# Logits of the dilated local attention by block-diagonal matmuls on TensorE in place of a key gather on GpSimd

## The chip, the cores and the metric

The kernel runs on one core of a Trainium2 chip. The metric is the device time of one execution in microseconds (us), the median of several runs. PE is TensorE (PEld its weight loads), DVE is VectorE, ACT is ScalarE, POOL is GpSimd and SP is the engine whose queue issues most DMAs. The profile is of one execution; the median comes from other executions.

## The reference

Two attention blocks over the same input of 2048 tokens and 512 columns, with 32 heads of 16, are mixed by a gate for each token. A is full attention. B looks at 8 keys a query: the query's own position and every second one before it.

```python
x = A_x
g = _sigmoid((x * gate_w).sum(-1, keepdims=True))
a = _A_ref(x, A_wqkv, A_wo)          # softmax(q k^T / 4) v, 32 heads, then @ wo
b = _B_ref(x, B_wqkv, B_wo)
return g * a + (1 - g) * b

# in _B_ref
W, dil = 8, 2
idx = pos[:, None] - off[None, :]    # off = arange(W) * dil
mask = idx >= 0
kg = k[:, :, idx_c, :].reshape(B, H, S, W, Dh)
vg = v[:, :, idx_c, :].reshape(B, H, S, W, Dh)
logits = jnp.einsum("bhsd,bhswd->bhsw", q, kg) * scale
logits = jnp.where(mask[None, None, :, :], logits, -1e9)
attn = _softmax(logits, axis=-1)
o = jnp.einsum("bhsw,bhswd->bhsd", attn, vg)
```

## The kernel before

**Attention A** fills most of the time. Its work is cut into 32 periods: 4 chunks of 512 queries (`QW`) by 8 groups of 4 heads. A period has 64 units, each one key tile of 128 by one head by 512 queries. Most units go in sets of 3 and 2 in turn: score matmuls into one of two PSUM rings (`qk`), one exponential on ACT over the set (`ex`, `pT<-ring`), then the product with the values on PE (`pv_run`). There are 1709 such units; "unit" below means one of them. Another 339 units have their exponentials on DVE (`d_set`): `p1` makes a 16-bit number from the PSUM score, and two adds over three units at once, `raise1` (1536 columns) and `raise2` (3072 columns), shift it in SBUF between four products. Their buffers are `pd_a` and, later, `wall`. PE also makes A's keys, queries and values from `xT`, and runs matmuls on a zero tile (`z`) where the order would leave it with little to do.

**Attention B** goes in 16 tiles of 128 tokens (`b_tile`, line 881). PE projects keys, values and queries of a tile (12 matmuls of 512 columns); DVE evicts keys and values into `kvs`, which SP writes to `kv_scr` in DRAM, and the queries, scaled, into `qb`. SP then loads, for each query in its partition, 4 of its 8 keys at a time (`ksh`), twice, and likewise the values (`vsh`). POOL makes the logits: 8 multiplications of 512 columns (`logits_mul`), three rounds of halving sums (`logits_add`) and a last sum (`logits_out`) for each pair of keys. The softmax follows: maximum on DVE (`sm_pre`), subtraction on POOL (`sm_sub`), exponential on ACT (`sm_exp`), sum and reciprocal on DVE (`sm_post`), the factor 1 - g and the product on POOL (`sm_gate`, `sm_mul`). POOL multiplies by the values (`av_mul`, 8 a tile), accumulating DMAs and POOL add the parts (`av_sum`, `av_last`), PE transposes the result (`fin`), and DVE writes it to `obt` (`oe`). For each chunk PE then multiplies `obt` and A's result by the two output matrices (`ab_part`), DVE evicts and SP writes the output.

**The order** of each engine is fixed when the program is built. `op` records every operation with an engine, an assumed length, a due time, what it depends on (`deps`), what it must follow (`after`), and the buffers it takes (`alloc`) and uses (`use`); `list_schedule` plays them through and writes out one order for each engine, which the engine then keeps. `CFG` gives B's due times: `b_start` and `b_space` place the tiles. So a wait of one instruction holds back all that stands behind it on its engine. Small PSUM results share three banks (`misc`). Every POOL, DVE, ACT and SP instruction is recorded by one helper, so the profile gives them all line 364, and most of PE's line 373; groups are told apart by the names of their tiles.

Of the kernel before, what the change touches and what calls it, by code (L numbers as in the profile page):

```python
# [21 lines left out]
    b_start=36.0,  # L22
    b_space=(43.0,) * 4 + (45.0,) * 4 + (47.0,) * 8,
# [17 lines left out]
NGA = 3  # L41
# [56 lines left out]
NPR = 3  # L98
# [21 lines left out]
FIN, QB, KB, WO = 52.0, 0.0, 0.0, 26.0  # L120
# [181 lines left out]
def kernel(  # L302
# [103 lines left out]
    for t in range(NT):  # L406
        BT.append(BT[-1] + cfg["b_space"][t])
    UNIT = 0.465
# [62 lines left out]
    kv_scr = tc.dram_tile([16 + S, 2 * D], BF16, name="kv_scr")  # L471
# [26 lines left out]
    omg = const.tile([128, NT], FP32, name="omg")  # L498
    e1, d1 = av[:, 1, 0:NT], av[:, 1, NT:2 * NT]
# [31 lines left out]
    def init_pool3():  # L531
        zst["z"] = work.tile([128, 2 * D], BF16, name="kvs", tag="kvs", bufs=2)
        G.memset(zst["z"][0:16, :], 0.0)
# [11 lines left out]
    def load_x(sc):  # L545
        def s():
            xl = work.tile([128, W // 2, D], BF16, name="xld", tag="gat", bufs=NGA) if sc < NGA else stage
# [25 lines left out]
    xtok = [tok("gat", NGA) if sc < NGA else tok("dt", NDT) for sc in range(NC)]  # L573
# [8 lines left out]
    o_bw = op("sp", 1.0, load_bw, -8.3, lat=19.0)  # L582
    o_zr = op("sp", 0.6, load_zero, -8.2, deps=[o_wz], use=[zt], lat=19.0)
# [287 lines left out]
    o_g = op("dve", 0.8, zgate, GT + 6, deps=[a])  # L871
    a = op("pe", 1.2, zrows, GT + 8, full=1, deps=[o_g, o_init_p], alloc=[tzr])
# [6 lines left out]
    HB = D  # L879

    def b_tile(t):
        st = {}
        tb = BT[t]
        cb, tl = t // TPC, t % TPC
        rel = max(24.0, tb - 70.0)

        def proj(key, off, c0):
            def s():
                if c0 == 0:
                    st[key] = misc_ps([128, D])  # L890
                    if key == "pk":
                        st["kvs"] = work.tile([128, 2 * D], BF16, name="kvs", tag="kvs", bufs=2)
                    if key == "pq":
                        st["qb"] = work.tile([128, D], BF16, name="qb", tag="qb", bufs=2)
                for c in range(c0, c0 + 2):
                    mm_ct(st[key], xT[:, c, t * 128:(t + 1) * 128], bw[:, c, off * D:(off + 1) * D], c == 0, c == DC - 1)
            return s
        tkv = tok("kvs", 2)

        def ke():  # L900
            V.tensor_copy(out=st["kvs"][:, 0:D], in_=st["pk"][:])

        def ve():
            V.tensor_copy(out=st["kvs"][:, D:2 * D], in_=st["pv"][:])

        def kvd():
            SP.dma_start(out=kv_scr[16 + t * 128:16 + (t + 1) * 128, :], in_=st["kvs"][:])
        tk = tok("misc", 2)
        a = op("pe", WAVE(2), proj("pk", 1, 0), tb - 34 - KB, full=2, deps=[o_bw] + o_xt[cb], alloc=[tk, tkv], rel=rel)
        a = op("pe", WAVE(2), proj("pk", 1, 2), tb - 33.5 - KB, full=2, deps=[a], use=[tk])  # L910
        ka = op("dve", 0.61, ke, tb - 33 - KB, deps=[a], use=[tk, tkv])
        tk = tok("misc", 2)
        a = op("pe", WAVE(2), proj("pv", 2, 0), tb - 32 - KB, full=2, deps=[o_bw] + o_xt[cb], alloc=[tk], rel=rel, after=[a])
        a = op("pe", WAVE(2), proj("pv", 2, 2), tb - 31.5 - KB, full=2, deps=[a], use=[tk])
        va = op("dve", 0.61, ve, tb - 31 - KB, deps=[a, ka], use=[tk, tkv])
        o_kvd.append(op("sp", 0.6, kvd, tb - 30 - KB, deps=[va], use=[tkv], lat=3.0))

        tqb = tok("qb", 2)

        def qe():  # L920
            V.tensor_scalar(out=st["qb"][:], in0=st["pq"][:], scalar1=float(DH) ** -0.5, scalar2=None, op0=ALU.mult)
        tk = tok("misc", 2)
        a = op("pe", WAVE(2), proj("pq", 0, 0), tb - 24 - QB, full=2, deps=[o_bw] + o_xt[cb], alloc=[tk, tqb], rel=rel)
        a = op("pe", WAVE(2), proj("pq", 0, 2), tb - 23.5 - QB, full=2, deps=[a], use=[tk])
        qa = op("dve", 0.61, qe, tb - 23 - QB, deps=[a], use=[tk, tqb])

        def load(key, off, hf):
            def s():
                r0 = 16 + t * 128 - DIL * hf * WH
                base = kv_scr[r0:r0 + 128, off * D:(off + 1) * D]  # L930
                st[key, hf] = work.tile([128, WH, D], BF16, name=key, tag="gat", bufs=NGA)
                SP.dma_start(out=st[key, hf][:], in_=_ap(base, [[2 * D, 128], [-DIL * 2 * D, WH], [1, D]]))
            return s
        tks, tvs = [tok("gat", NGA), tok("gat", NGA)], [tok("gat", NGA), tok("gat", NGA)]
        tlg, tbb = tok("lg", 2), tok("obb", 1)
        kvd_ = o_kvd[max(0, t - 1):t + 1] + [o_zr]
        lk = [op("sp", 0.7, load("ksh", 0, hf), tb + KL[hf], deps=kvd_, alloc=[tks[hf]], lat=7.0) for hf in range(2)]
        lv = [op("sp", 0.7, load("vsh", 1, hf), tb + (18, 30)[hf], deps=kvd_, alloc=[tvs[hf]], lat=7.0) for hf in range(2)]

        def logits_mul(hf, wp, w_, c0):  # L940
            def s():
                if hf == 0 and wp == 0 and w_ == 0 and c0 == 0:
                    st["lg"] = work.tile([128, H, W], FP32, name="lg", tag="lg", bufs=2)
                if w_ == 0 and c0 == 0:
                    st["prod", hf, wp] = work.tile([128, WP, D], FP32, name="prod", tag="prod", bufs=NPR)
                G.tensor_tensor(out=st["prod", hf, wp][:, w_, c0:c0 + HB], in0=st["ksh", hf][:, wp + w_, c0:c0 + HB],
                                in1=st["qb"][:, c0:c0 + HB], op=ALU.mult)
            return s, "bb", HB

        def logits_add(hf, wp, n, w0, ws):  # L950
            def s():
                pv_ = st["prod", hf, wp][:].rearrange("p w (h d) -> p w h d", d=DH)
                G.tensor_tensor(out=pv_[:, w0:w0 + ws, :, 0:n], in0=pv_[:, w0:w0 + ws, :, 0:n],
                                in1=pv_[:, w0:w0 + ws, :, n:2 * n], op=ALU.add)
            return s, "ff", ws * H * n

        def logits_out(hf, wp):
            def s():
                lg = st["lg"]
                pv_ = st["prod", hf, wp][:].rearrange("p w (h d) -> p w h d", d=DH)  # L960
                w0 = hf * WH + wp
                G.tensor_tensor(out=lg[:, :, w0:w0 + WP].rearrange("p h w -> p w h"),
                                in0=pv_[:, :, :, 0], in1=pv_[:, :, :, 1], op=ALU.add)
# [87 lines left out]
        def chain_ops(seq, dls, alloc, toks):  # L1051

            made, tps, a, seen = {}, {}, None, set()
            for n_, (g_, k_, (f, kind, n), src, deps) in enumerate(seq):
                new = g_ not in tps
                if new:
                    tps[g_] = tok("prod", NPR)
# [432 lines left out]
```

## Time and profile before

| what | value |
|---|---|
| median of 3 runs | 842.53 us (841.78 to 843.44) |
| the profiled execution's own time | 844.3 us |
| its span, first to last instruction | 842.5 us |
| mean granted TensorE clock | 0.985 |
| first exponential of A begins | 19.54 us |
| ACT, exponentials of A (684) | 782.0 us |
| DVE / POOL busy | 668.4 / 669.4 us |
| PE matmuls on the zero tile | 403 |
| DMA queue of SP: packets, MB | 52,752, 54.05 |

The span lies within the profiled execution's time. Busy times of PE come from matmuls that overlap, so they are not added up as shares. An instruction's idle time stands with the group that waited, and behind the arrow stands what ended the wait. Since all engines keep a written order, an idle time shows where the order and the real lengths part.

### The profile page before, as it was taken

To read this page: it belongs to the slowest core of one execution; us is meant where nothing else is said; L and a number is where in the kernel's file an instruction comes from. 1 tells how busy PE (TensorE), PEld (TensorE's weight loads), DVE (VectorE), ACT (ScalarE), POOL (GpSimd) and SP (SyncE) were. 2 spreads that over 40 slices of the span, in tenths; PEclk is the share of its full clock that TensorE was granted. 3 is DMA by queue.
4 is the path that set the end of the run, shared out by engine and by line. 5 is a ranking of instruction groups with operands and counts; after the bars stand their busy time and mean duration, and the time that the engine had idled before them with its cause. 6 is when DMAs were issued, how large, how long until landed. Compare 5 with 4: busy or idle time off the path is not lost.

```text
span 842.5 us, 17539 instructions
## 1 busy us (share of the span) xinstructions
PE 763.5 (91%) x6947; PEld 243.6 (29%) x7000; DVE 668.4 (79%) x967; ACT 789.7 (94%) x706; POOL 669.4 (79%) x710
## 2 busy tenths in 40 slices
PE   8999899998989888998899998989989999999996
PEld 4333333233222222222222222222222222223322
DVE  5556987868775788999988689988788889887775
ACT  3999989997999899999999999999989999999995
POOL 3197979998799885799979998988898996999400
PEclk9999999998999899999999999999999999999998
DMA  7402171534361705236042625342342516120000
GB/s 252 139 29 86 36 179 58 132 103 87 98 153 55 171 2 101 88 113 162 27 120 69 167 60 139 86 125 67 91 86 88 138 38 166 48 76 2 1 2 25
DMA packets 58882, 77.18 MB, mean 92 GB/s; under 512 B 3744, under 2 KB 50848, under 8 KB 58800
## 3 DMA queue, kind: packets, MB, share of 16 engines
q1 hardware_dynamic: 52752, 54.05, 20.6%
q0 software_dynamic: 6048, 22.02, 14.1%
q8 instruction: 54, 0.88, 0.5%
q14 instruction: 28, 0.23, 0.1%
HBM read 43.78 MB, written 10.26 MB: 64 GB/s over the span
## 4 chain that ended last, share of the span: by engine, by line
ACT 38%; PE 29%; issue 17%; DVE 14%; DMA 1%; ACTq 0%; SPq 0%; DVEq 0%
ACT pT L364 37%; PE misc_ps L373 20%; PE ring L373 8%; DVE pd_a L364 6%; DVE wall L364 6%; DMA xld<-in_A_x_dram 1%; DVE qa L364 1%; DVE kvs L364 0%; PE pxt L621 0%; DVE kt_all L364 0%; DVE vd_all L364 0%; DVE qs L364 0%; DVE vp_all L364 0%; ACT lg L364 0%; DVE qb L364 0%
## 5 line engine op out<-in xcount | busy, mean ns | idle before, releaser
L364 ACT ACTIVATE pT<-ring 128x1536 bf16<-128x1536 f32 (+1 forms) x684 | 782.0, 1289 | 35.2 <-PE ring L373 28.2
L373 PE MATMUL ring<-qt,kt_all 32*128 32x512 bf16 x1709 | 273.2, 385 | 39.2 <-ACT pT L364 32.5
L373 PE MATMUL misc_ps<-pT,vp_all 128*17 128x512 bf16 (+1 forms) x1709 | 217.2, 387 | 0.4
L364 POOL TENSOR_TENSOR prod<-ksh,qb 128x512 f32<-128x512 bf16 x128 | 170.9, 1364 | 41.4 <-DMA ksh<-kv_scr 34.0
L364 POOL TENSOR_TENSOR prod<-prod 128x512 f32<-128x512 f32 (+2 forms) x192 | 187.6, 977 | 3.2
L373 PEld LDWEIGHTS <-kt_all 32*128 32x128 bf16 x2048 | 85.7, 91 | 299.1 <-issue 290.6
L364 DVE TENSOR_SCALAR pd_a<-pd_a 128x1536 uint16<-128x1536 uint16 (+1 forms) x130 | 153.4, 1180 | 15.3 <-PE misc_ps L373 14.2
L364 DVE TENSOR_SCALAR pd_a<-misc_ps 128x512 uint16<-128x512 f32 x195 | 130.6, 680 | 39.7 <-PE misc_ps L373 36.8
L373 PE MATMUL misc_ps<-z 128*32 128x512 bf16 x403 | 133.4, 393 | 1.9 <-DVE z L364 1.6
L364 DVE TENSOR_SCALAR wall<-wall 128x1536 uint16<-128x1536 uint16 x96 | 121.5, 1271 | 16.8 <-PE misc_ps L373 16.2
L373 PE MATMUL misc_ps<-qt,kt_all 32*128 32x512 bf16 x339 | 124.9, 384 | 7.6 <-DVE pd_a L364 4.4
L364 DVE TENSOR_SCALAR wall<-misc_ps 128x512 uint16<-128x512 f32 x144 | 95.4, 682 | 17.4 <-PE misc_ps L373 13.5
L373 PEld LDWEIGHTS <-vp_all 128*17 128x17 bf16 (+1 forms) x2048 | 57.8, 88 | 85.9 <-issue 70.0
L364 POOL TENSOR_TENSOR prod<-vsh,lg 128x512 f32<-128x512 bf16 x64 | 80.8, 1326 | 0.0
L373 PE MATMUL misc_ps<-pd_a,vd_all 128*17 128x512 bf16 x585 | 73.1, 384 | 7.3 <-DVE pd_a L364 7.1
L364 POOL TENSOR_TENSOR av<-vsh,lg 128x512 f32<-128x512 bf16 x64 | 79.4, 1269 | 0.1
L373 PE MATMUL misc_ps<-wall,vd_all 128*17 128x512 bf16 x432 | 54.5, 386 | 9.7 <-DVE wall L364 9.5
L373 PEld LDWEIGHTS <-vd_all 128*17 128x17 bf16 x1017 | 32.0, 88 | 75.3 <-issue 70.0
L373 PE MATMUL misc_ps<-bw,xT 128*128 128x512 bf16 x163 | 50.0, 383 | 2.3 <-issue 1.6
L373 PEld LDWEIGHTS <-z 128*32 128x32 bf16 x403 | 35.7, 97 | 48.4 <-issue 27.1
L373 PE MATMUL misc_ps<-xT,wall 128*32 128x512 bf16 x544 | 39.8, 381 | 0.0
L373 PEld LDWEIGHTS <-xT 128*128 128x128 bf16 x576 | 29.5, 97 | 34.0 <-issue 29.1
(88 smaller groups left out, 581.3 us busy)
## 6 DMA issues: line engine op xcount, KB each, us to landing
ksh<-kv_scr SPq DMA_DIRECT2D x32, 512.0 KB
vsh<-kv_scr SPq DMA_DIRECT2D x32, 512.0 KB
av<-prod POOLq DMA_DIRECT2D x28, 512.0 KB, 5.4
av<-av POOLq DMA_DIRECT2D x14, 512.0 KB, 4.9
kv_scr<-kvs SPq DMA_DIRECT2D x16, 256.0 KB
qt<-q_scr SPq DMA_DIRECT2D x30, 128.0 KB
out_dram<-osb SPq DMA_DIRECT2D x16, 128.0 KB
q_scr<-qs SPq DMA_DIRECT2D x15, 128.0 KB
```

What stands on the lines that cost most here:

```text
L364: return chain_on(key, f(*a, **k))
L373: return chain(nc.tensor.matmul(out, lhsT=lhsT, rhs=rhs, start=start, stop=stop, **kw))
```

## The change

The keys are no longer loaded for each query. B now works in units of one chunk of 512 tokens by 8 heads (16 units, `scores_of`). PE projects keys and queries with heads and head columns on the partitions; DVE writes the keys into `kt_b`, where POOL puts the last 14 columns of the chunk before in front (`pad`, `keep`), and the scaled queries into `qb`. Eight DMAs copy each head's 16 partitions into its place of `q_bd`, a tile that holds zeros elsewhere. A block of 16 queries of one parity by 8 heads is then one matmul of 128 columns against 32 keys of that parity: of its 32 x 16 logits a head, those where the key is one of the query's 8 lie on a band. DVE evicts 16 blocks at a time (`ev`), writes zeros into the gaps, and SP writes them to `lg_scr` in DRAM with a row length that makes the band a fixed stride, so that one DMA reads, for 128 queries, 8 keys by 8 heads in pieces of 8 numbers (`lget`). Softmax and values stay as they were, with three differences: a tile now holds the tokens of one parity of half a chunk, in an order by block, so the values come in 8 DMAs of 128 rows and `oe` writes with a stride; the logits lie as chunk of heads, key, head; and 1 - g is taken through DRAM into that order (`gput`, `gget`). Values are projected tile by tile as before (`v_rows`). The due times of all B's steps are new, the output of a chunk waits for all four of its tiles, and there are two gather buffers for three, two product buffers for three.

```diff
     set_sizes=(3, 2),
     n_dve=(3, 3, 6, 6, 6, 9, 9, 9) + (12,) * 24,
     dve_tiles=4,
-    b_start=36.0,
-    b_space=(43.0,) * 4 + (45.0,) * 4 + (47.0,) * 8,
+    b_start=128.4,
+    b_space=(29.0, 29.0, 29.0, 58.1, 40.2, 40.2, 40.2, 66.3, 40.2, 40.2, 40.2, 55.5, 40.2, 40.2, 40.2, 40.0),
+    l_start=(63.6, 197.6, 372.0, 585.9),
+    l_step=(12.1, 16.2, 16.2, 16.2),
+    v_start=(65.3, 199.3, 373.7, 587.6),
+    v_step=(10.9, 14.6, 14.6, 14.6),
     chain=("pe", "dve", "act", "pool", "sp"),
 )
 
...
@@ -38,7 +42,7 @@
 NV = 4
 NGR = 3
 NPT = 3
-NGA = 3
+NGA = 2
 LATE0 = 8
 NDT = 2
 NCB = 2
...
-NPR = 3
+NPR = 2
+KP, BLK = 14, 136
+ROWL = 8 * BLK - 8
...
-FIN, QB, KB, WO = 52.0, 0.0, 0.0, 26.0
+FIN, WO = 17.0, 26.0
...
-    kv_scr = tc.dram_tile([16 + S, 2 * D], BF16, name="kv_scr")
+    kv_scr = tc.dram_tile([16 + S, D], BF16, name="kv_scr")
+    lg_scr = tc.dram_tile([NC * DC, 128 * ROWL], FP32, name="lg_scr")
...
+    q_bd = const.tile([128, 8, QW], BF16, name="q_bd")
+    kt_b = const.tile([128, 2, KP + QW + 18], BF16, name="kt_b")
+    k_end = const.tile([128, DC, KP], BF16, name="k_end")
...
+    def scores_of(cb, c):
+
+        st = {}
+        un = DC * cb + c
+        dl = LT[un]
+        rel = max(24.0, dl - 30.0)
+        kt = kt_b[:, un % 2]
+
+        def proj(key, off, c0):
+            def s():
+                if c0 == 0:
+                    st[key] = misc_ps([128, QW])
+                for kc in range(c0, c0 + 2):
+                    mm_ct(st[key], bw[:, kc, off * D + c * 128:off * D + (c + 1) * 128], xT[:, kc, cb * QW:(cb + 1) * QW],
+                          kc == 0, kc == DC - 1)
+            return s
+
+        def pad():
+            G.tensor_copy(out=kt[:, 0:KP], in_=k_end[:, c])
+
+        def ke():
+            V.tensor_copy(out=kt[:, KP:KP + QW], in_=st["pk"][:])
+
+        def keep():
+            G.tensor_copy(out=k_end[:, c], in_=kt[:, QW:QW + KP])
+
+        def qe():
+            st["q"] = work.tile([128, QW], BF16, name="qb", tag="qb", bufs=1)
+            V.tensor_scalar(out=st["q"][:], in0=st["pq"][:], scalar1=float(DH) ** -0.5, scalar2=None, op0=ALU.mult)
+
+        def diag(h0):
+            def s():
+                for h in range(h0, h0 + 4):
+                    r_ = slice(DH * h, DH * (h + 1))
+                    SP.dma_start(out=q_bd[r_, h, :], in_=st["q"][r_, :])
+            return s
+        tkk, tqd, tqe = tok("ktb", 2), tok("qbd", 1), tok("qb", 1)
+        tk = tok("misc", 2)
+        kd = []
+        if cb:
+            kd.append(op("pool", 0.2, pad, GFIRST, deps=[o_end[un - DC]], alloc=[tkk], after=o_kt[-1:]))
+            o_kt.append(kd[-1])
+        a = op("pe", WAVE(2), proj("pk", 1, 0), dl - 12, full=2, deps=[o_bw] + o_xt[cb], alloc=[tk], rel=rel)
+        a = op("pe", WAVE(2), proj("pk", 1, 2), dl - 11.5, full=2, deps=[a], use=[tk])
+        a = op("dve", 0.61, ke, dl - 11, deps=[a, o_zb], alloc=[] if cb else [tkk], use=[tk] + ([tkk] if cb else []), after=o_kt[-1:])
+        if not cb:
+            o_kt.append(a)
+        kd.append(a)
+        o_end.append(op("pool", 0.2, keep, GFIRST, deps=[a] + kd[:-1], use=[tkk]))
+        tk = tok("misc", 2)
+        a = op("pe", WAVE(2), proj("pq", 0, 0), dl - 10, full=2, deps=[o_bw] + o_xt[cb], alloc=[tk], rel=rel)
+        a = op("pe", WAVE(2), proj("pq", 0, 2), dl - 9.5, full=2, deps=[a], use=[tk])
+        a = op("dve", 0.61, qe, dl - 9, deps=[a], alloc=[tqe], use=[tk])
+        dg = []
+        for h0 in (0, 4):
+            dg.append(op("sp", 2.0, diag(h0), dl - 8 + h0 / 4, deps=[a, o_zb], after=dg[:], alloc=[] if h0 else [tqd], use=[tqe] + ([tqd] if h0 else []), lat=4.2))
+        q_v = q_bd[:].rearrange("p h (b q e) -> p b e q h", q=16, e=2)
+
+        def blocks(g, u0):
+            def s():
+                if u0 == 0:
+                    st["s", g] = misc_ps([128, TPC, 128])
+                for u in range(u0, u0 + 2):
+                    for j in range(TPC):
+                        e, b = j // 2, 8 * (j % 2) + 4 * g + u
+                        k0 = 32 * b + e
+                        mm(st["s", g][32 * j:32 * j + 32, u, :].rearrange("p (q h) -> p q h", h=8), kt[:, k0:k0 + 63:2],
+                           q_v[:, b, e], True, True, tile_position=(0, 32 * j))
+            return s
+        tse = tok("sev", 1)
+
+        def ev(g):
+            def s():
+                if g == 0:
+                    st["e"] = work.tile([128, 8, BLK], FP32, name="sev", tag="sev", bufs=1)
+                V.tensor_copy(out=st["e"][:, 4 * g:4 * g + 4, 0:128], in_=st["s", g][:])
+                if g == 0:
+                    V.memset(st["e"][:, 0:7, 128:BLK], 0.0)
+                if cb == 0 and g == 0:
+                    for j in (0, 2):
+                        V.memset(st["e"][32 * j:32 * j + W - 1, 0, 0:128], NEG)
+            return s
+
+        def put():
+            SP.dma_start(out=_ap(lg_scr[un:un + 1, 0:1], [[ROWL, 128], [1, ROWL]]),
+                         in_=st["e"][:].rearrange("p u n -> p (u n)")[:, 0:ROWL])
+        es = []
+        for g in range(2):
+            tk = tok("misc", 2)
+            a = None
+            for u0 in (0, 2):
+                a = op("pe", 0.0, blocks(g, u0), dl + 2 * g + 0.5 * u0, mode="c", js=list(range(TPC)) * 2, full=0.5,
+                       deps=([a] if u0 else []) + dg + kd, alloc=[] if u0 else [tk],
+                       use=[tkk, tqd] + ([tk] if u0 else []))
+            es.append(op("dve", 0.7 if g else 0.8, ev(g), dl + 2 + 2 * g, deps=[a] + es, alloc=[] if g else [tse], use=[tk] + ([tse] if g else [])))
+        o_lgw.setdefault(cb, []).append(op("sp", 0.6, put, dl + 6, deps=es, use=[tse], lat=3.5))
 
...
+        def lget():
+            st["lg"] = work.tile([128, DC, W, 8], FP32, name="lg", tag="lg", bufs=2)
+            for c in range(DC):
+                r0 = 32 * (t % TPC) * ROWL
+                SP.dma_start(out=st["lg"][:, c], in_=_ap(lg_scr[DC * cb + c:DC * cb + c + 1, r0:r0 + 1], [[BLK, 128], [ROWL, W], [1, 8]]))
+
+        def load(hf):
+            def s():
+                st["vsh", hf] = work.tile([128, WH, D], BF16, name="vsh", tag="gat", bufs=NGA)
+                for w_ in range(WH):
+                    r0 = 16 + cb * QW + 256 * hb + e - DIL * (W - 1 - hf * WH - w_)
+                    SP.dma_start(out=st["vsh", hf][:, w_, :], in_=_ap(kv_scr[r0:r0 + 1, :], [[2 * D, 16], [32 * D, 8], [1, D]]))
+            return s
+        kvd_ = o_kvd[max(0, TPC * cb - 1):TPC * (cb + 1)] + [o_zr]
+        l1 = op("sp", 2.0, lget, tb - 8, deps=o_lgw[cb], alloc=[tlg], lat=9.0)
+        lv = [op("sp", 2.0, load(hf), tb - 6 + 8 * hf, deps=kvd_, alloc=[tvs[hf]], lat=7.0) for hf in range(2)]
+        loads["k", t], loads["v", t] = [], lv
 
...
-            V.tensor_copy(out=obt_tiles[cb][:, :, tl * 128:(tl + 1) * 128], in_=st["ptp"][:])
+            o_ = obt_tiles[cb][:, :, 256 * hb:256 * (hb + 1)].rearrange("p c (b q e) -> p c e q b", q=16, e=2)[:, :, e]
+            V.tensor_copy(out=o_, in_=st["ptp"][:].rearrange("p c (q b) -> p c q b", q=16))
...
-                   deps=[a] if k0 else [o_oat[NG * c_ + ng - 1], o_wo] + o_obt[t:t + 1],
+                   deps=[a] if k0 else [o_oat[NG * c_ + ng - 1], o_wo] + o_obt[TPC * c_:TPC * (c_ + 1)],
```

More of the change, by code (lines that the diff above doesn't have):

```diff
@@ L531, in init_pool3 @@
     def init_pool3():
[L532 removed]
+        zst["z"] = work.tile([128, D], BF16, name="kvs", tag="kvs", bufs=2)
         G.memset(zst["z"][0:16, :], 0.0)
@@ L879, with v_rows, proj, ve @@
     HB = D
+    o_lgw = {}
+    def v_rows(t):
+        st = {}
+        cb = t // TPC
+        dl = VT[t]
+        def proj(c0):
+            def s():
+                if c0 == 0:
+                    st["pv"] = misc_ps([128, D])
+                    st["kvs"] = work.tile([128, D], BF16, name="kvs", tag="kvs", bufs=2)
+                for c in range(c0, c0 + 2):
+                    mm_ct(st["pv"], xT[:, c, t * 128:(t + 1) * 128], bw[:, c, 2 * D:3 * D], c == 0, c == DC - 1)
+            return s
+        def ve():
+            V.tensor_copy(out=st["kvs"][:], in_=st["pv"][:])
+        def kvd():
+            SP.dma_start(out=kv_scr[16 + t * 128:16 + (t + 1) * 128, :], in_=st["kvs"][:])
+        tk, tkv = tok("misc", 2), tok("kvs", 2)
+        rel = max(24.0, dl - 40.0)
+        a = op("pe", WAVE(2), proj(0), dl - 1, full=2, deps=[o_bw] + o_xt[cb], alloc=[tk, tkv], rel=rel)
+        a = op("pe", WAVE(2), proj(2), dl - 0.5, full=2, deps=[a], use=[tk])
+        a = op("dve", 0.61, ve, dl, deps=[a], use=[tk, tkv])
+        o_kvd.append(op("sp", 0.6, kvd, dl + 1, deps=[a], use=[tkv], lat=3.0))
@@ L920, in qe @@
[L920 to L948, printed above, removed]
```

162 lines of the change are left out of this document (56 added, 106 removed).

## The prediction

> **What bounds the kernel now.** I read the busy times first, then the stages, then the groups by shape, then one stall in order of time. The busy times name ACT:
>
> ```profile
> PE 763.5 (91%) x6947; PEld 243.6 (29%) x7000; DVE 668.4 (79%) x967; ACT 789.7 (94%) x706; POOL 669.4 (79%) x710
> ```
>
> The stages (width; busy us of PE, PEld, DVE, ACT, POOL; clock; DMA share; GB/s) show where ACT is not busy:
>
> ```profile
> 100.00:200.00 100.00, 92.67 (x963) 33.60 (x968) 80.31 (x132) 94.66 (x86) 90.42 (x98) 1.00 0.48 119
> 200.00:300.00 100.00, 88.48 (x678) 25.27 (x682) 71.23 (x90) 90.42 (x81) 89.56 (x99) 0.93 0.43 106
> 300.00:400.00 100.00, 89.60 (x782) 26.32 (x788) 91.97 (x124) 98.15 (x88) 79.34 (x80) 1.00 0.38 97
> 600.00:700.00 100.00, 91.20 (x777) 26.41 (x778) 83.28 (x110) 96.16 (x87) 92.06 (x92) 0.98 0.37 92
> 700.00:790.00 90.00, 84.04 (x743) 26.00 (x743) 76.35 (x100) 89.94 (x82) 78.38 (x74) 1.00 0.25 67
> ```
>
> Between 20 and 790 us all stages together leave ACT 29.6 us idle. The other idle time is the start (first exponential at 19.5 us) and the tail, which the change leaves alone. So at most 29.6 us are to be had. What makes them? The groups by shape (busy us, mean ns):
>
> ```profile
> L364 DVE TENSOR_SCALAR pd_a<-pd_a 128x3072 uint16<-128x3072 uint16 x65 | 87.7, 1349 | 14.5 <-PE misc_ps L373 14.2
> L364 DVE TENSOR_SCALAR wall<-wall 128x3072 uint16<-128x3072 uint16 x48 | 73.2, 1524 | 16.4 <-PE misc_ps L373 16.2
> L364 DVE TENSOR_SCALAR pd_a<-pd_a 128x1536 uint16<-128x1536 uint16 x65 | 65.7, 1011 | 0.8
> L364 DVE TENSOR_SCALAR wall<-wall 128x1536 uint16<-128x1536 uint16 x48 | 48.8, 1017 | 0.4
> ```
>
> and the same from 795 us on, where POOL has ended:
>
> ```profile
> L364 DVE TENSOR_SCALAR wall<-wall 128x3072 uint16<-128x3072 uint16 x4 | 3.8, 956 | 2.4 <-PE misc_ps L373 2.4
> L364 DVE TENSOR_SCALAR wall<-wall 128x1536 uint16<-128x1536 uint16 x4 | 2.2, 556 | 0.1
> ```
>
> Beside a busy POOL these raises take longer by 65 x 0.455 + 48 x 0.461 + 65 x 0.393 + 48 x 0.568 = 104.5 us in all. One of them in order of time, with POOL's work beside it and what followed:
>
> ```profile
> 101.74 3.46 DVE L364 TENSOR_SCALAR pd_a<-pd_a 128x3072 uint16<-128x3072 uint16 x1 [0.28 <-PE misc_ps L373]
> 101.94 2.43 POOL L364 TENSOR_TENSOR prod<-vsh,lg 128x512 f32<-128x512 bf16 x2
> ...
> 105.25 0.39 PE L373 MATMUL misc_ps<-pd_a,vd_all 128*17 128x512 bf16 x3 [1.51 <-DVE pd_a L364]
> ...
> 108.36 2.36 ACT L364 ACTIVATE pT<-ring 128x1536 bf16<-128x1536 f32 x2 [3.18 <-PE ring L373]
> ```
>
> A raise of 0.96 us took 3.46, PE waited in order for it, and ACT lost 3.18. So ACT bounds, and POOL's load takes part of ACT's time by way of DVE and PE.
>
> **What it removes.** On POOL: 128 multiplications (170.9 us), their 192 halving sums (86.6 + 60.3 + 40.6) and 64 last sums (25.0): 383.4 of 669.4 us, which leaves 286. On SP and the queues: 32 loads of keys, 16.8 MB.
>
> **What it adds on POOL.** 28 copies of 14 columns at about 0.2 us (the `perm` copy of 48 columns: 0.214) and two memsets of 5,184 columns (0.54 us for 544 columns), before the first exponential and beside DMA waits: 6 + 5 = 11 us. POOL comes to 297 us, 0.444 of before. I take the raises' excess to go with POOL's load: 104.5 falls to 46 us.
>
> **On DVE.** 32 evictions of 512 f32 columns (fa, the same shape, 0.69 us): 22 us; 24 memsets at 0.06: 1.4; the 16 `oe` copies now write with a stride, at most 0.69 for 0.41: 4.5. Together 28 us, under the 58 that the raises give back. Without that cover they would cost up to 28. On ACT nothing changes in kind or number.
>
> **On PE.** Projections keep their count (192 of 512 columns). New are 512 block matmuls of 128 columns in 64 groups of eight. Eight `xT,wall` matmuls of 512 columns start within 0.43 us; a quarter of the columns gives 0.11, and with a change of array mode (about 0.11 between groups) and weight loads I take 0.25 a group, 16 us. The queries are read with a stride, which no row shows: the other end is the full 512-column price, 0.54 a group, 35 us. I take 0.25, as the rows nearest in columns say. The order has 374 fillers (z matmuls) for 403; a second matmul in a row adds 0.215 (two `bwo,obt` take 0.60, one 0.385), so 6 us come back. The load is bunched: projections and blocks stand within units 80-235, 368-513, 695-865 and 1128-1325 of 1709 (a unit is 512 columns of exponentials, 0.477 us). That is 318 us holding 192 x 0.215 + 16 = 57 us of work, 18%, where before the projections were 5% all along; fillers (87 us) and idle (79 us) gave PE 20% of room. It fits on the average; not where A's key and value projections stand too, near units 110-235. There I charge one more stall like the 3.2 us above, and 1.3 us for a few late blocks: 4.5 us. Ends: 0 and 20.
>
> **On SP and DMA.** A unit issues 8 copies onto the diagonal and one write, a tile 4 reads of logits and 8 loads of values. The loads of A's queries stand in the same queue; they are ordered some 20 us ahead of use. Copies of 16 rows (`woarr`) issue in 0.545 us each, and a `kv_scr` write let its reader start 1.8 us after its issue. From query eviction to blocks: 0.69 + 0.1 + 8 x 0.545 + 1.8 = 6.95 us, while the order leaves 15 to 40 units, 7.2 us at the least. So no wait; behind it would stand the next score matmuls, and ACT. The reads are 65,536 pieces of 32 bytes. The gate vector's 512 pieces of 2 bytes moved 288 packets in 0.2 us over 16 engines, 11 ns each: 256 an engine make 2.8 us a tile, 4.6 landed. The maximum on DVE that waits for them, with the raises queued behind it, stands 10 to 47 units later (4.8 to 22 us). Ends: 0 and 2 us for the first tile of each chunk, 8 in all; I take 0.
>
> [...]
>
> **The sum.** ACT's 29.6 us idle times 0.556, the part of POOL's load that goes, is 16.5 us (ends: 0, if raises are not what stalls ACT; 29.6, all). From the profiled execution's 844.3 us (span 842.5 and 1.8 around it): 844.3 - 16.5 + 4.5 = 832.3. The median of the runs is 842.5, 1.8 below that execution: **830.5 us**.
>
> **The rivals.** *Slower: the diagonal lands late.* Place: the first block matmul of each of 16 units, in PE's order. If the chain takes 11 us instead of 6.95 (issues of 1.3 to 1.4 us, as SP shows in its first 10 us when the queues are full, would do it), the waits against the 16 leads (eight are 15 to 18 units) add to 26 us: 844.3 - 16.5 + 4.5 + 26 - 1.8 = 856. It outweighs the gain from about 9.5 us on. Against it: later issues have medians of 0.37 and 0.58 us. *No gain: raises are not the cause.* From 700 to 790 us POOL is 87% busy and ACT loses 0.06 us; PE, with 93 fillers there against 21 from 100 to 200 us, takes the delays up. If PE's room decides, the bunches give back what POOL's rest wins: 844.3 + 4.5 - 1.8 = 847, or with half the gain 839. *More gain.* The clock fell to 0.57 at 205-210 us after such waits; if the raises' excess and these falls vanish together and the bunches fit, 842.5 - 25 = 818. *It does not do what it says:* POOL could keep its load only through slower multiplications by the logits, whose layout changes; twice their 160 us would leave POOL at 457, and the gain at 9: 838.
>
> **Chances.** Forecast 0.50 (own range 822 to 839); more gain 0.08; no or half gain 0.20; late diagonal 0.20; slower multiplications 0.02. This kernel's measurement tells 0.2% (1.7 us) from no change. Of the third, 0.05 is faster, 0.05 the same, 0.10 slower. Faster: 0.50 + 0.08 + 0.02 + 0.05 = 0.65; same 0.05; slower 0.10 + 0.20 = 0.30. The range takes in both sides: 818 to 854.
>
> **What would show it.** Right: POOL near 300 us, raises near 750 and 1150 ns, ACT idle about 17 us in the stages, no PE wait on q_bd or kt_b above 0.5 us. Wrong: PE waiting for a DMA into q_bd; a block group above 0.5 us; DVE waiting for lg; raises as long as before; a lower clock in the bunches.

## The result, and the profile after

The kernel after takes 888.22 us (median of 4 runs, 885.19 to 892.26) beside 842.99 us for the kernel before (4 runs): a ratio of 1.052, with a 95% interval of 1.045 to 1.059. The forecast was 830.5 us and faster. The profiled execution took 888.7 us, with a span of 886.7 us against 842.5. Beside the experiments below, the kernel before had medians of 841.87 to 845.08 us, so times of different experiments can be compared to about 3 us. One of the four executions of e4, at 877.6 us, was in a slower state: it is in the median below but not in the ratio, and without it the median is 862.23 us.

The busy times of the kernel after:

```profile
PE 803.9 (91%) x7426; PEld 259.8 (29%) x7483; DVE 658.4 (74%) x1023; ACT 803.5 (91%) x706; POOL 315.6 (36%) x355
```

POOL fell from 669.4 to 315.6 us, as the change meant it to. But ACT, which bounds, is busy 13.8 us longer, and PE 40.4. The same stages as before (width; busy us of PE, PEld, DVE, ACT, POOL; granted clock; DMA share; GB/s):

```profile
100.00:200.00 100.00, 95.47 (x1077) 36.43 (x1084) 73.66 (x143) 91.75 (x81) 29.58 (x34) 1.00 0.32 71
200.00:300.00 100.00, 88.15 (x756) 28.16 (x763) 69.09 (x100) 86.12 (x75) 43.03 (x49) 0.93 0.54 121
300.00:400.00 100.00, 90.14 (x723) 24.62 (x733) 80.46 (x114) 90.55 (x81) 36.95 (x42) 0.93 0.38 80
600.00:700.00 100.00, 93.12 (x832) 27.40 (x839) 79.82 (x119) 93.30 (x82) 33.77 (x40) 0.97 0.41 98
700.00:790.00 90.00, 79.93 (x695) 23.93 (x695) 68.86 (x100) 87.19 (x80) 47.04 (x49) 0.98 0.42 86
```

ACT is busy less than before in every one of them. In the first stage PE has the full clock and is 95% busy; in the second and third the clock is 0.93. Over the whole span the granted clock is 0.966, against 0.985 before. The groups by shape (busy us, mean ns; then idle time before):

```profile
L370 DVE TENSOR_SCALAR pd_a<-pd_a 128x3072 uint16<-128x3072 uint16 x65 | 73.1, 1125 | 9.8 <-PE misc_ps L379 9.7
...
L379 PE MATMUL misc_ps<-q_bd,kt_b 128*32 128x128 bf16 x512 | 55.3, 493 | 8.1 <-DMA vsh<-kv_scr 2.9 <-DVE pd_a L370 2.6 <-DMA q_bd<-qb 1.3
...
L370 DVE TENSOR_SCALAR wall<-wall 128x3072 uint16<-128x3072 uint16 x48 | 51.3, 1068 | 17.0 <-PE misc_ps L379 17.0
L370 DVE TENSOR_SCALAR pd_a<-pd_a 128x1536 uint16<-128x1536 uint16 x65 | 45.9, 706 | 0.7
...
L370 DVE TENSOR_SCALAR wall<-wall 128x1536 uint16<-128x1536 uint16 x48 | 38.8, 809 | 0.5
L370 DVE COPY obt<-misc_ps 128x512 bf16<-128x512 bf16 x16 | 38.4, 2397 | 1.0 <-PE misc_ps L1184 1.0
```

The raises became short: against 0.956 and 0.556 us in the kernel before from 795 us on, where POOL has ended, their excess is 65 x 0.169 + 48 x 0.112 + 65 x 0.150 + 48 x 0.253 = 38 us, against 104.5 before. Two other rows are out of line. The `oe` copy has 2,397 ns, where the kernel before had 414:

```profile
L364 DVE COPY obt<-misc_ps 128x512 bf16<-128x512 bf16 x16 | 6.6, 414 | 3.0 <-PE misc_ps L1125 3.0
```

A block matmul of 128 columns has 493 ns, though the `ident,obb` matmuls, also of 128 columns, have 221; the eight blocks of a group start 53.7 ns apart on the average. One `oe` copy in order of time:

```profile
201.59 2.39 DVE L370 COPY obt<-misc_ps 128x512 bf16<-128x512 bf16 x1
...
204.03 0.38 PE L379 MATMUL misc_ps<-z 128*32 128x512 bf16 x1 [1.28 <-DVE obt L370]
...
205.05 1.02 ACT L370 ACTIVATE pT<-ring 128x1024 bf16<-128x1024 f32 x1 [0.99 <-PE misc_ps L379]
...
207.21 2.36 ACT L370 ACTIVATE pT<-ring 128x1536 bf16<-128x1536 f32 x2 [1.14 <-PE ring L379]
```

PE waits in its order for the bank that the copy frees, then ACT loses 0.99 and 1.14 us; between 200 and 210 us the clock is 0.72. An exponential beside blocks, and the blocks:

```profile
401.53 2.08 ACT L370 ACTIVATE pT<-ring 128x1536 bf16<-128x1536 f32 x1 [0.70 <-PE ring L379]
```

```profile
401.59 0.91 PE L379 MATMUL misc_ps<-q_bd,kt_b 128*32 128x128 bf16 x8
...
402.73 0.92 PE L379 MATMUL misc_ps<-q_bd,kt_b 128*32 128x128 bf16 x8 [0.23 <-DVE pd_a L370]
```

This exponential of 1536 columns took 2.08 us; the mean of all 342 in the kernel before is 1.50. Taken one by one in the trace, the 34 exponentials of 1536 columns beside blocks (a block starts during them or up to 0.2 us ahead) have 1,713 ns and the other 308 have 1,496; for 1024 columns it is 1,227 (26) and 1,073 (315). That is 34 x 0.217 + 26 x 0.154 = 11.4 us on the engine that bounds, without any wait.

The exponentials before and after:

```profile
L364 ACT ACTIVATE pT<-ring 128x1536 bf16<-128x1536 f32 x342 | 513.1, 1500 | 30.9 <-PE ring L373 26.0 <-PE misc_ps L373 3.9 <-ACT pT L364 0.3
L364 ACT ACTIVATE pT<-ring 128x1024 bf16<-128x1024 f32 x341 | 367.6, 1078 | 4.3 <-PE ring L373 2.2 <-PE misc_ps L373 1.8
```

```profile
L370 ACT ACTIVATE pT<-ring 128x1536 bf16<-128x1536 f32 x342 | 519.0, 1518 | 43.5 <-PE ring L379 32.0 <-PE misc_ps L379 9.7
L370 ACT ACTIVATE pT<-ring 128x1024 bf16<-128x1024 f32 x341 | 369.9, 1085 | 17.2 <-PE ring L379 9.2 <-PE misc_ps L379 7.8
```

The span's 44.2 us more divide as follows: the first exponential at 22.3 us instead of 19.5 (2.8); from the last one to the end 10.6 instead of 8.5 (2.0); between them 853.8 instead of 814.4 us (39.3). Of these, 25.5 is ACT's idle time before exponentials and 13.8 its longer busy time: 8.2 from the two groups' busy times, and the rest because the two overlap less.

### The profile page after: what moved, and what is told of

It reads as the page before. It is cut to its first block, busy times and chain, and to the rows that moved or that the text cites. A ratio compares the mean times of both kernels' runs of the same rounds, so it can differ in the third digit from the quotient of the medians.

```text
span 886.7 us, 18724 instructions
## 1 busy us (share of the span) xinstructions
PE 803.9 (91%) x7426; PEld 259.8 (29%) x7483; DVE 658.4 (74%) x1023; ACT 803.5 (91%) x706; POOL 315.6 (36%) x355
## 3 DMA queue, kind: packets, MB, share of 16 engines
q0 software_dynamic: 6048, 22.02, 13.6%
## 4 chain that ended last, share of the span: by engine, by line
PE 43%; ACT 26%; DVE 14%; issue 12%; SPq 3%; DMA 2%; DVEq 0%; ACTq 0%; POOL 0%
PE misc_ps L379 30%; ACT pT L370 26%; PE ring L379 12%; DVE pd_a L370 4%; SPq L370 3%; DVE obt L370 3%; DVE wall L370 3%; DMA q_bd<-qb 1%; DVE qb L370 1%; DMA wall<-in_A_wqkv_dram 1%; DVE accT L370 1%; PE pxt L642 0%; DVE osb L370 0%; DVE kvs L370 0%; DVE vp_all L370 0%
## 5 line engine op out<-in xcount | busy, mean ns | idle before, releaser
L370 ACT ACTIVATE pT<-ring 128x1536 bf16<-128x1536 f32 (+1 forms) x684 | 795.3, 1301 | 60.7 <-PE ring L379 41.2
L379 PE MATMUL misc_ps<-pT,vp_all 128*17 128x512 bf16 (+1 forms) x1709 | 224.4, 392 | 1.7 <-DVE rden L370 1.1
L370 DVE TENSOR_SCALAR pd_a<-misc_ps 128x512 uint16<-128x512 f32 x195 | 133.9, 693 | 53.2 <-PE misc_ps L379 50.1
L379 PE MATMUL misc_ps<-z 128*32 128x512 bf16 x374 | 126.1, 400 | 3.7 <-DVE obt L370 2.1
L370 DVE TENSOR_SCALAR pd_a<-pd_a 128x1536 uint16<-128x1536 uint16 (+1 forms) x130 | 118.6, 915 | 10.5 <-PE misc_ps L379 9.7
L370 DVE TENSOR_SCALAR wall<-misc_ps 128x512 uint16<-128x512 f32 x144 | 98.6, 698 | 27.5 <-PE misc_ps L379 25.5
L370 DVE TENSOR_SCALAR wall<-wall 128x1536 uint16<-128x1536 uint16 x96 | 89.6, 938 | 17.5 <-PE misc_ps L379 17.0
L370 POOL TENSOR_TENSOR rden<-rden,g_rw 128x16 f32<-128x16 f32 x30 | 9.7, 322 | 185.3 <-DVE rden L370 185.3
L379 PE MATMUL misc_ps<-q_bd,kt_b 128*32 128x128 bf16 x512 | 55.3, 493 | 8.1 <-DMA vsh<-kv_scr 2.9
L370 DVE COPY sev<-misc_ps 128x512 f32<-128x512 f32 x32 | 24.0, 750 | 25.8 <-PE misc_ps L379 25.7
L370 POOL TENSOR_SCALAR rr<-rr,omg 128x32 f32<-128x32 f32 x16 | 7.6, 473 | 93.5 <-DVE rr L370 62.2
```

The costliest lines, as they stand in the source:

```text
L370: return chain_on(key, f(*a, **k))
L379: return chain(nc.tensor.matmul(out, lhsT=lhsT, rhs=rhs, start=start, stop=stop, **kw))
```

## The experiments

The theory after the first reading had four parts: the relief of POOL works as forecast; the `oe` copies cost about 25 us; the blocks' strided read costs PE and ACT some 10 to 25; the rest is a late start and a denser order. The rival was that raises never were what stalls ACT, and that PE's scarce room swallows everything.

**The relief alone (e1).** In the kernel before:

```diff
-    G.tensor_tensor(out=st["prod", hf, wp][:, w_, c0:c0 + HB], in0=st["ksh", hf][:, wp + w_, c0:c0 + HB],
-                    in1=st["qb"][:, c0:c0 + HB], op=ALU.mult)
+    G.tensor_tensor(out=st["prod", hf, wp][:, w_, :].rearrange("p (h d) -> p h d", d=DH)[:, :, 0:2],
+                    in0=st["ksh", hf][:, wp + w_, :].rearrange("p (h d) -> p h d", d=DH)[:, :, 0:2],
+                    in1=st["qb"][:].rearrange("p (h d) -> p h d", d=DH)[:, :, 0:2], op=ALU.mult)
...
 def logits_add(hf, wp, n, w0, ws):
     def s():
+        if n > 1:
+            return
```

> The kernel before, with most of the work for its logits on POOL left out: each multiplication makes 64 of its 512 columns and the three halving sums a product are not made, so the logits are a sum of 2 of 16 products; the order of all other work is kept. POOL comes to about 350 us from 669. It does alone what the change does to POOL. Theory (relief, the forecast's first step): raises fall to about 0.75 and 1.15 us, ACT's idle time between 20 and 790 us falls from 29.6 to about 15 us, time about 828 us (822 to 833). Rival (PE's room decides, the raises are not what stalls ACT): raises fall as well, but ACT's idle time stays at 27 to 30 us, and the time is 840 to 843 us.

Measured: 823.45 us against 843.02, ratio 0.978 (0.971 to 0.986). Its busy times, and the raises that were the longest before:

```profile
PE 753.2 (92%) x6947; PEld 244.0 (30%) x7000; DVE 602.4 (73%) x967; ACT 787.1 (96%) x706; POOL 375.3 (46%) x518
```

```profile
L364 DVE TENSOR_SCALAR wall<-wall 128x3072 uint16<-128x3072 uint16 x48 | 50.4, 1050 | 20.3 <-PE misc_ps L373 20.0
```

POOL at 375 us instead of 669 shortens these raises from 1,524 to 1,050 ns, and ACT's idle time in the stages from 20 to 790 us falls from 29.6 to 11.0 us. Between the two, the waits of PE's products for the raised numbers fall from 16.6 to 4.1 us (the kernel before, then e1):

```profile
L373 PE MATMUL misc_ps<-pd_a,vd_all 128*17 128x512 bf16 x585 | 73.1, 384 | 7.3 <-DVE pd_a L364 7.1
...
L373 PE MATMUL misc_ps<-wall,vd_all 128*17 128x512 bf16 x432 | 54.5, 386 | 9.7 <-DVE wall L364 9.5
```

```profile
L373 PE MATMUL misc_ps<-pd_a,vd_all 128*17 128x512 bf16 x585 | 73.5, 382 | 3.2 <-DVE pd_a L364 3.0
...
L373 PE MATMUL misc_ps<-wall,vd_all 128*17 128x512 bf16 x432 | 54.4, 384 | 1.1 <-DVE wall L364 1.1
```

The rival falls: raises lengthened by POOL were what stalled ACT, and the gain of 19.6 us is a little above the 16.5 of the forecast, with POOL less relieved than the forecast's 297 us. So the kernel after lost some 65 us elsewhere.

**The copy, added to the kernel before and mended in the kernel after (e2, e3).** e2 gives the kernel before the strided write:

```diff
-    V.tensor_copy(out=obt_tiles[cb][:, :, tl * 128:(tl + 1) * 128], in_=st["ptp"][:])
+    o_ = obt_tiles[cb][:, :, 256 * (tl // 2):256 * (tl // 2 + 1)].rearrange("p c (b q e) -> p c e q b", q=16, e=2)[:, :, tl % 2]
+    V.tensor_copy(out=o_, in_=st["ptp"][:].rearrange("p c (q b) -> p c q b", q=16))
```

> The kernel before, with nothing changed but the place to which the 16 oe copies write: with the 64-byte stride of the kernel after (so the local branch's rows come out in another order). Each copy takes 2.39 us in the kernel after against 0.41 in the kernel before; 16 of them add 32 us to DVE. Theory (DVE's order holds up PE, PE then ACT): about half to all of it reaches the end, 857 to 874 us from 842.5, with PE waiting for obt in its rows. Rival (DVE, 79% busy, takes it up in its idle time of 174 us): 842 to 846 us.

e3 swaps the loops in the kernel after, so that every element goes where it went:

```diff
-    o_ = ....rearrange("p c (b q e) -> p c e q b", q=16, e=2)[:, :, e]
-    V.tensor_copy(out=o_, in_=st["ptp"][:].rearrange("p c (q b) -> p c q b", q=16))
+    o_ = ....rearrange("p c (b q e) -> p c e b q", q=16, e=2)[:, :, e]
+    V.tensor_copy(out=o_, in_=st["ptp"][:].rearrange("p c (q b) -> p c b q", q=16))
```

> The kernel after, with the loops of the oe copy swapped: the same elements to the same places, but the innermost loop writes every second element (4 bytes apart) instead of every 32nd (64 bytes). Order of all work kept. If the 64-byte stride is what makes the copy 2.39 us, a copy falls to 0.7 us or less. Theory (the copy costs the end what it holds up): 888 falls by 15 to 28 us, to 860 to 873. Rival (what stalls ACT is PE's load in the bunches, the copies only lie beside it): the copies fall as much, the time stays at 883 to 890 us.

e2: 867.52 us, ratio 1.031 (1.024 to 1.039); e3: 862.78 us, ratio 1.024 (1.018 to 1.031), 25.4 below the kernel after. The copies, of e2 and then of e3:

```profile
L364 DVE COPY obt<-misc_ps 128x512 bf16<-128x512 bf16 x16 | 38.4, 2403 | 2.9 <-PE misc_ps L1125 1.5 <-PE misc_ps L373 1.4
```

```profile
L370 DVE COPY obt<-misc_ps 128x512 bf16<-128x512 bf16 x16 | 12.0, 748 | 1.1 <-PE misc_ps L1184 1.1
```

The same elements cost 2,400 ns with writes 64 bytes apart and 748 with writes 4 bytes apart. In e2 only the writes differ from the kernel before, so their stride is what takes the copy from 414 to 2,403 ns. In e3 the swap also makes the copy's reads of PSUM 16 bytes apart instead of contiguous, so which of the two strides keeps it above 414 ns is not shown. 31.8 us more on DVE cost the kernel before 24.5 at the end, and 26.4 fewer gave the kernel after 25.4. DVE is idle a fifth to a quarter of the time and yet absorbs little: the copy stands in an order in which PE's next bank waits for it. In e2 PE waits 17.3 us for the copy itself, in 14 places; the rest reaches the end through what stands behind the copy on DVE, which is not taken apart here. On ACT the whole effect is idle time: in e3 its busy time stays (803.1 for 803.5 us), and its idle time before exponentials falls from 60.7 to 33.5 us.

**The blocks' read (e4).** In the kernel after:

```diff
-    q_v = q_bd[:].rearrange("p h (b q e) -> p b e q h", q=16, e=2)
+    q_v = q_bd[:].rearrange("p h (b q e) -> p b e h q", q=16, e=2)
-    mm(st["s", g][...].rearrange("p (q h) -> p q h", h=8), kt[:, k0:k0 + 63:2],
+    mm(st["s", g][...].rearrange("p (q h) -> p h q", h=8), kt[:, k0:k0 + 63:2],
```

> The kernel after, with the 128 columns of a block matmul read in another order: innermost 16 queries 4 bytes apart, then 8 heads, instead of innermost 8 heads 1024 bytes apart; its result in PSUM is written with the same permutation, so the values and their places stay. Order of all work kept. Theory (the strided read is what makes a group of eight 0.44 us or more, and slows the exponentials beside it): mean 493 ns falls to 250 or so, the time falls by 8 to 16 us, to 872 to 880. Rival (the stride of the read is not the cause, or the blocks fit into PE's room): mean or time unchanged, 885 to 890 us.

Measured: 864.62 us, ratio 1.025 (1.016 to 1.034), 23.6 below the kernel after and more than expected. Its runs lie between 860.15 and 877.60 us, so the 23.6 is good to a few us. Blocks now start 13.4 ns apart, a quarter of 53.7. An exponential beside them, and the blocks' row:

```profile
384.45 1.45 ACT L370 ACTIVATE pT<-ring 128x1536 bf16<-128x1536 f32 x1 [1.08 <-PE ring L379]
```

```profile
L379 PE MATMUL misc_ps<-q_bd,kt_b 128*32 128x128 bf16 x512 | 25.8, 298 | 7.4 <-DMA kv_scr<-kvs 2.8 <-DVE pd_a L370 2.1 <-POOL k_end L370 1.3
```

The exponential stands beside 16 blocks as the one of 2.08 us did, and takes 1.45. Over the trace the 1536-column exponentials beside blocks have 1,494 ns, the others 1,498: the extra 11.4 us on ACT are gone, and PE has 512 x 40.3 ns = 20.6 us back. ACT's busy time falls by 12.1 us to 791.4, and its idle time before exponentials by 15.5 to 45.2. DVE's evictions of the blocks go with it, from 750 to 691 ns.

**The same read with no part of the change (e11, e12).** To show that the read alone lengthens exponentials, 252 fillers of the kernel before were replaced:

```diff
...
-    mm(tz[0:32, :], z32[:], z_bc, True, True, tile_position=(0, 0))
+    for j in range(4):
+        mm(tz[32 * j:32 * j + 32, 0:128], z32[:], far, True, True, tile_position=(0, 32 * j))
```

`far` is 128 elements of `bw`, with the inner loop 8 elements 1024 bytes apart (e11) or 16 elements 4 bytes apart (e12).

> The kernel before, no part of the change in it. From 60 us of the plan on, each of 252 filler matmuls (zeros times a row, into a bank that nobody reads) is replaced by four on the four row groups with 128 columns each, whose moving operand is read from B's weights as the blocks read the queries: innermost 8 elements 1024 bytes apart. By the blocks' spacing of 53.7 ns four take 0.215 us, what one filler takes now, so PE's plan holds. Theory (the read 1024 bytes apart is what makes PE four times slower and the exponentials beside it some 200 ns longer, whoever else is there): spacing near 54 ns, exponentials beside these fillers 150 to 270 ns longer than the others, 850 to 875 us. Rival (the longer exponentials come from something else of the blocks' surroundings, as DVE's evictions or DMA): exponentials within 30 ns of the others, time within 5 us of 843.

> The same replacement in the kernel before with the loops of the read swapped: innermost 16 elements 4 bytes apart, then 8 rows of 1024 bytes. The same number of matmuls, columns and weight loads. Theory: spacing near 13.4 ns, exponentials beside the fillers within 30 ns of the others, time 835 to 845 us (less PE time, but the clock may fall without the fillers' work). Rival (it is the number of small matmuls, not their stride): as slow as with 1024 bytes.

e11: 907.32 us against 841.87, ratio 1.076 (1.065 to 1.086); e12: 843.48 us, ratio 1.001 (0.996 to 1.006). The exponentials and the new fillers, of e11 and then of e12:

```profile
L364 ACT ACTIVATE pT<-ring 128x1536 bf16<-128x1536 f32 x342 | 544.7, 1593 | 57.6 <-PE ring L373 30.0 <-PE misc_ps L373 26.2 <-ACT pT L364 0.2
...
L373 PE MATMUL misc_ps<-bw,z 128*32 128x128 bf16 x1008 | 134.5, 496 | 0.0
```

```profile
L364 ACT ACTIVATE pT<-ring 128x1536 bf16<-128x1536 f32 x342 | 517.6, 1513 | 27.7 <-PE ring L373 21.6 <-PE misc_ps L373 5.0 <-ACT pT L364 0.2
...
L373 PE MATMUL misc_ps<-bw,z 128*32 128x128 bf16 x1008 | 61.5, 225 | 0.2 <-DVE accT L364 0.2
```

Of the 1536-column exponentials of e11, those with fewer than four of these fillers beside them have 1,502 ns, those with four to seven 1,737, and with twelve and more 1,930; in e12 it is 1,500, 1,533 and 1,579. The read 1024 bytes apart slows both PE and ACT, in a kernel without blocks, diagonal or logits in DRAM. But in e12 the exponentials beside the fillers are still 33 to 79 ns longer than the others, more than the 30 expected, and nothing here shows why. The cost at the end, 65 us, was beyond the expected range: the fillers are many more than the blocks, and ACT alone is busy 35 us longer (824.7 for 789.7).

**Both loop orders, and the start (e5, e6).** e5 joins e3 and e4. In e6 the diagonal is also cleared on DVE:

```diff
...
 def init_bd():
     G.memset(kt_b[:], 0.0)
-    G.memset(q_bd[:], 0.0)
+def init_qd():
+    V.memset(q_bd[:], 0.0)
...
+o_zq = op("dve", 2.2, init_qd, -8.95, deps=[o_init_d])
...
```

The copies onto the diagonal then wait for DVE's memset in place of POOL's (`o_zq` for `o_zb`), and POOL's memset is planned at 1.0 us for 5.0.

> The kernel after with both loop orders of the last runs: the oe copy writing every second element, and the block matmuls reading 16 queries inside of 8 heads. Alone the first took 25.4 us off the 888.2, the second 23.6. If the two losses are separate (DVE's order on the one side, PE's spacing and the slowed exponentials on the other), both come off: 839 us, between 835 and 843, within 1% of the kernel before. Rival (both work through the same scarce room on PE, so that taking one away already gives back most): 850 to 858 us.

> The same as the kernel with both loop orders, and the memset of the diagonal moved from POOL, where it lay at 6.2 to 9.7 us beside DVE's copies, to DVE itself, behind its first memsets, where DVE waits for the first loads (1.5 to 6.1 us). The first exponential comes back from 22.3 to 23.4 us to the 19.5 of the kernel before: 3 to 4 us less than the kernel with both loop orders, about 835.5 us. Rival (the later start comes from the loads, not from POOL's memset): first exponential still after 22 us, no gain.

e5: 839.86 us against 843.69, ratio 0.996 (0.993 to 1.000). The two losses add, within the spread of the runs: 25.4 + 23.6 = 49.0 expected, 48.4 measured. The granted clock comes back with them: 0.966 in the kernel after, 0.987 in e3, 0.983 in e4 and 0.995 in e5. What part of the two losses goes by way of the clock is not separated here. e6: 839.10 us, ratio 0.997 (0.994 to 1.000). First what stood in the way in the kernel after (start, duration), then e6's memset (min, median and max ns; start):

```profile
6.24 3.68 DVE L370 COPY wall<-wall 128x64 bf16<-128x64 bf16 x2 [4.68 <-DMA wall<-in_A_wqkv_dram]
6.26 3.50 POOL L370 MEMSET q_bd<- 128x4096 bf16 x1
...
6.63 3.29 DVE L370 COPY xT<-pxt 128x1024 bf16<-128x1024 bf16 x1
```

```profile
L370 DVE MEMSET q_bd<- x1: 1765/1765/1765, 1.9 to 1.9; 128x2048 uint32 x1
```

The copies of 64 columns, 0.64 us for two in the kernel before, end at 9.92 us, just behind POOL's memset at 9.76. Moved to DVE it takes 1.77 us in a pause, and the first exponential stands at 19.7 us instead of 22.5. So the cause of the late start is shown, but the end gains nothing that can be told: e6 loses 1.3 us to a new stall at 40.6 us, and waits 3.6 us for the diagonal against 0.4 in e5. The expected gain was wrong.

**The diagonal's lead (e8).** The forecast's slower rival, put to e5:

```diff
 for h in range(h0, h0 + 4):
     r_ = slice(DH * h, DH * (h + 1))
-    SP.dma_start(out=q_bd[r_, h, :], in_=st["q"][r_, :])
+    for q0 in (0, QW // 2):
+        SP.dma_start(out=q_bd[r_, h, q0:q0 + QW // 2], in_=st["q"][r_, q0:q0 + QW // 2])
```

> The kernel with both loop orders, with each of the 8 copies of a unit onto the diagonal split into two of half the columns: 16 issues of about 0.55 us instead of 8, so that the chain from the query eviction to the blocks is some 4.5 us longer, and nothing else. This asks for the forecast's rival of the late diagonal. Theory (the order's leads of 7.2 us and more cover the chain, only a few units wait): within 3 us of the kernel with both loop orders, PE's waits for q_bd under 5 us in all. Rival (the leads are just used up): each of 16 units waits 1 to 4 us, 15 to 40 us more.

Measured: 915.95 us, ratio 1.087 (1.082 to 1.092), 76 above e5. One place, and the sum over the trace (waiting <- waited for: us, times, longest):

```profile
262.17 1.48 PE L379 MATMUL misc_ps<-q_bd,kt_b 128*32 128x128 bf16 x16 [6.41 <-DMA q_bd<-qb]
...
264.30 1.45 ACT L370 ACTIVATE pT<-ring 128x1536 bf16<-128x1536 f32 x1 [7.14 <-PE ring L379]
```

```profile
PE misc_ps L379 <- DMA q_bd<-qb: 57.4, 20, 6.4
```

The theory was wrong and the rival right, though the cost was beyond the rival's 15 to 40 us: the leads hold, with little to spare. In the trace 13 of the 16 units have their first block wait for `q_bd`, by 1.9 to 6.4 us. On the average a unit costs 76 / 16 = 4.8 us, about all that eight more issues of 0.59 us add.

**Other orders (e7, e9, e10).** All three build on e6. e7 plans with measured durations, e9 also with the diagonal's, e10 with the diagonal's alone:

```diff
-    free[j] = t0 + PASS                                # e7, e9
+    free[j] = t0 + o.pas                               # 0.06 for blocks, else 0.22
-    o_obt.append(op("dve", 0.34, oe, ...))             # e7, e9
+    o_obt.append(op("dve", 0.75, oe, ...))
-    dg.append(op("sp", 2.0, diag(h0), ..., lat=4.2))   # e9, e10
+    dg.append(op("sp", 2.45, diag(h0), ..., lat=6.5))
```

> The kernel with the three changes, its order planned again with the durations that the traces show: the block matmuls at 0.06 us a row group instead of 0.22, the oe copy at 0.75 instead of 0.34. If an order made for wrong durations is what still keeps it above the 823.5 us of the kernel before with POOL relieved, it comes to 825 to 832. Rival (the rest is the bunched work itself): within 3 us of the kernel with the three changes.

> The kernel with the three changes and the order planned with measured durations, and the copies onto the diagonal planned at what they take (2.45 us for four issues instead of 2.0, landed after 6.5 instead of 4.2), so that the blocks stand later behind them. The order without this let PE wait 5.1 us for q_bd in three places, with ACT losing 3.2 and 2.3 us behind the first of them. Theory (short leads are the most of what is left): q_bd waits under 1 us, 829 to 834 us against 836.4. Rival (the order only moves the stalls): 835 to 840.

> The kernel with the three changes and the old durations for blocks and oe copies, with only the copies onto the diagonal planned at 2.45 and 6.5 us: the order has the slack of the blocks' too long plan and longer leads. If the leads matter and the blocks' plan does not, as fast as the kernel with all durations measured, 829 to 836; if the measured block and copy durations were what gave the 2.7 us between 839.1 and 836.4, it stays at 837 to 840.

Measured: e7 836.38 us, ratio 0.994 (0.991 to 0.997); e9 843.90 against 845.08, ratio 0.999 (0.995 to 1.004); e10 835.24, ratio 0.992 (0.988 to 0.996). e7 and e10 are faster than both kernels, if by little: e10 by 0.8% of the kernel before. e7 misses its 825 to 832 us and stays within 3 us of e6, as its rival said. e9 misses both its ranges: it holds both corrections and is not faster than the kernel before. Its ten runs spread from 837.45 to 848.49 us, and its profiled execution, at 838.56, is near the short end, so the trace does not show what made the others longer. That a new order moves the stalls by as much as it mends fits, but is not shown. None of the three came near e1's 823. That e10 is best for its longer leads is not shown either.

## Why the prediction was wrong

*What bounds, and what relief is worth: right.* ACT bounds. POOL came to 315.6 us (forecast 297), the raises' excess to 38 (forecast 46), and e1, with POOL at 375 us, gave 19.6 us where the sum had 16.5.

*The step that failed on DVE:* "the 16 `oe` copies now write with a stride, at most 0.69 for 0.41: 4.5". The mechanism was seen and its size taken from a row without a stride, which was no bound. It measured 2.40 us a copy, 31.8 us in all, and 25.4 at the end. "Together 28 us, under the 58 that the raises give back" failed with it, as a reason to charge nothing: DVE's sum did fall, by 10 us, but the time of an engine is no cover for one instruction that another waits for. A smaller term was left out: the maximum and sum over strided logits take 610 ns instead of 405, 32 x 0.205 = 6.6 us. The 0.69 us of the blocks' evictions was right by itself: they took 0.75 us beside the strided read, and 0.69 in e4 and e5 without it.

*The step that failed on PE:* "I take 0.25, as the rows nearest in columns say". The other end, 0.54, was the right one: eight blocks 53.7 ns apart are 0.43 us, ahead of the 0.11 that the forecast put on the change of array mode, and the read with a stride, "which no row shows", was the reason. Even so the forecast charged 4.5 us for all of PE, because it set the work against PE's average room.

*The step that failed on ACT:* "On ACT nothing changes in kind or number". Nothing did, and yet 60 exponentials took 11.4 us longer beside the strided blocks. No row of before could show it; it went unbounded. With what PE's own spacing adds to ACT's waits it makes the 23.6 us of e4: about 12 us of ACT's busy time and 15 of its idle time in the trace.

*The start:* "two memsets ... before the first exponential and beside DMA waits". They were beside DVE's copies and held them for 3.5 us. At the end this was worth less than can be told.

*SP and DMA: the charge of 0 was right, its reason was not.* The blocks waited 1.3 us for `q_bd` and DVE 0.8 us for the logits in the whole kernel. But the forecast called leads of "7.2 us at the least" against 6.95 "no wait" and did not say how steep the edge is; e8 shows it. In the kernel after the eight issues of a unit took 4.9 to 7.0 us, where the forecast had 8 x 0.545 = 4.4. The logits' reads were priced about right: their 65,536 packets of 32 bytes took 9.0 ns each on the mean (forecast 11), and the four reads of the tile issued from 186.88 us had landed at 191.65, 4.8 us later (forecast 4.6). The rate was low, 131 KB in 2.65 us, and the leads covered all of it but DVE's 0.8 us. The charge of 0 holds for this order alone: in e7, e9 and e10 DVE waits 7.3, 6.8 and 5.0 us for the logits.

*The sum.* Without both strides e5 stands at 839.9, 9.4 above the forecast. Against e1's profiled execution its span is 13.2 us longer: 3.0 before the first exponential, 2.0 behind the last, and 8.2 between, where ACT's idle time before exponentials is 23.1 us against 16.6. The 4.5 charged for the bunches is near these 6.5 us more of idle time, but that the bunches make them is not shown. Why the saved start is lost again, and which order would keep it, is open.

## What to carry to other kernels

When a change gives an operand a stride, price it by its stride and not by its shape alone: the same copy cost 0.41, 0.75 and 2.40 us with its writes 2, 4 and 64 bytes apart (at 0.75 its reads were strided too), and the same matmuls started 13 or 54 ns apart with their moving operand read in steps of 4 or 1024 bytes. Here two loops of the access pattern were swapped, with the data where they are, and the copy came from 2.40 to 0.75 us and the matmuls from 54 ns apart to 13. And bound what a neighbour does to the bounding engine: beside the strided blocks an unchanged exponential took 1,713 ns on the mean instead of 1,496.

## What the runs showed of the hardware

PE reading its moving operand 1024 bytes apart made ACT's exponentials, which read PSUM and write SBUF, up to 0.4 us longer (1,930 against 1,502 ns in e11); read 4 bytes apart it was 1,579 against 1,500 (e12). DVE's evictions became longer too: beside four and more of e11's fillers the `p1` evictions into `pd_a` took 850 ns (36 of them) against 682 (158), and in e12 681 against 680. What it is that the engines share there is not shown. DVE's copies beside POOL's memset of `q_bd` in the kernel after ended just behind it, at 9.92 us behind 9.76: the two of 64 columns took 3.68 us together, against 0.64 in the kernel before, and one of `xT` 3.29, against 0.68.

The two slow accesses of the change stepped by 64 and by 1024 bytes; with steps of 4 bytes the `oe` copy went from 2,397 to 748 ns (e3) and the blocks from 53.7 ns apart to 13.4 (e4). The matmuls are then at the rate of the `xT,wall` matmuls of the kernel before, where four of 512 columns start every 0.217 us, 13.6 ns for a quarter of one. The copy is not at its 414 ns, and what keeps it from there is open, as its PSUM reads changed as well. Writing PSUM in steps of 32 bytes did not keep the blocks of e4 from starting 13.4 ns apart.
